# Eight lists of tiles in place of six, and three chains of a scan and two expert layers rearranged between VectorE, ScalarE and GpSimd

## The chip, the cores and the metric

The kernel runs on one core of a Trainium2 chip. The metric is the device time of one execution in microseconds (us), the median of several runs. TensorE (PE) does matrix products, VectorE (DVE) and ScalarE (ACT) elementwise work and the emptying of PSUM, GpSimd (POOL) the scatters of rows, SyncE (SP) issues the other transfers.

## The reference

Three stages follow each other over 2 sequences of 5056 positions with 256 features, 10,112 rows in all. All is float32.

```python
log_a = c * sig_r * np.log(np.clip(a_base, 1e-06, 1.0 - 1e-06))[None, None, :]
a_t = np.exp(log_a)
norm = np.sqrt(np.maximum(1.0 - a_t * a_t, 1e-06))
x_gated = norm * sig_i * x
for t in range(S):
    h = a_t[:, t] * h + x_gated[:, t]
    y[:, t] = h
...
logits = x @ w_gate + modality_bias[modality_id]
e_idx = np.argmax(logits, axis=1)
...
for e in range(E):
    h = np.maximum(x[mask] @ w1[e], 0.0)
    out[mask] = gate_w[mask, None] * (h @ w2[e])
```

The second expert layer is the same without the modality bias. Each has 8 experts of 256 x 1024 and 1024 x 256, and each row goes to one expert; `gate_w` is that expert's softmax probability.

## The kernel before

The scan goes in ten chunks of 512 positions (the last has 448). For a chunk, two halves of 128 features lie on the partitions, and each step runs per half `k` and sequence `b`: ScalarE takes tanh of both gates (L413), the decay (L416), its square (L425) and the root (L433); VectorE clamps in between (`rest`, L430), forms the gated input (`gated`, L419), multiplies it by the root (`mul`, L436) and scans (`scan`, L440). TensorE then turns each of the eight tiles of 128 tokens and multiplies it by the router's weights in the same pass (`rows`, L461), into one of two PSUM buffers. `copy` (L471 on ScalarE, L473 on VectorE; the list `act` says which tile goes to ScalarE) brings the tile's row to SBUF, and `take` (L481) adds the two partial logits of each expert. `route` picks the expert (`pick`, L341) and the place among that expert's tokens (`rank`, L359, with products on TensorE), and `send` (L494) scatters each row, with its number and gate, to the expert's region of a DRAM tensor X1 by an indirect DMA from GpSimd (L219).

Layer 1 works in slots, one for each 256 rows of one expert. A slot loads its rows (`load_rows`), turns them (`transposes`, L904; the copies L905 and L906 make a high and a low half), and runs six points: four of `ffn1` (L915 to L917, emptied by ScalarE as hTh, L919, and by VectorE as the low half hTl, L920) and two of `ffn2` (L929 to L931). Three PSUM buffers `ph` serve `ffn1`. After it, `end_steps` scales the rows by the gate (L941), routes them for layer 2 with `pick` and `rank`, and scatters them to X2. Its steps stand beside the next slot's points. Where the slot two before had another expert, the weights come from DRAM into a ring of five stages and are split into high and low halves (`split`, L878 and L879) during the slot before; there are two weight sets, for even and odd slots. Layer 2 has the same slots without routing.

Which expert a slot serves is settled on the chip. `phases` cuts layer 1 into lists: after so many chunks (`CUTS`) as many slots are listed as whole tiles are sure to be there. `plan_steps` is the plan of a list, 29 small steps of VectorE that count whole tiles for each expert and give each slot its expert, its first row and whether the weights change. Layer 1 has 40 regular slots.

The order is written out by hand. A slot has six ticks, the first slot begins at tick 45 (`T0`), and `STEPS` gives for each chunk the ticks, counted from its start, at which its steps are recorded; what is marked early stands ahead of the slot's point, the rest behind it. The starts of the first three chunks are given. The loop over lists gives the others: a list's last chunk must be sent before its first slot's rows are loaded, chunks keep 12 ticks apart, and starts that are left are spread evenly:

```python
s = max(start[-1] + PACE, LOAD2 + 2 if c + i == 2 else 0, start[c - 1] + (by - start[c - 1]) * (i + 1) // n)
start.append(next(x for x in [s - d for d in range(POINTS)] + [s + d for d in range(POINTS)] if x - start[-1] >= PACE and fits(x, c + i) and x >= LOAD2 + 2))
```

## Time and profile before

| what | value |
|---|---|
| median of 3 runs | 1179.78 us (1169.88 to 1182.34) |
| the profiled execution | 1184.67 us |
| its span in the trace | 1182.9 us |
| TensorE at work | 1093.8 us |
| mean granted TensorE clock | 0.968 of full speed |
| moved by DMA | 133.76 MB |

A row of busy times gives a stretch of the span, its length, and for PE, PEld (the loading of weights into TensorE), DVE, ACT and POOL the busy us with the number of instructions; then the granted clock, the mean busy share of the DMA engines and GB/s. Where a row is of some instructions alone, engines without any are left out. A row of waits says which engine, tensor and line stood idle, and after the arrow what ended it. Durations overlap a little where short instructions follow each other.

### The profile page before, as it was taken

The page shows a single profiled execution, that of the slowest core. Times are in us where ns is not written, and L with a number is a line of the kernel's source. Part 1 is how long each engine was busy: PE and PEld are TensorE (multiplying, and loading weights), DVE is VectorE, ACT ScalarE, POOL GpSimd, SP SyncE. Part 2 cuts the span into 40 slices and gives each one's busy share as a digit, 9 for nine tenths or more (in the row PEclk, how much of TensorE's full clock was granted, in tenths as well). Part 3 has the DMA queues.
Part 4 walks back from the last instruction along what each step waited for, and adds up shares of the span by engine and source line. Part 5 has one row for each costly group of instructions (what it writes and reads, how often), then busy time and mean ns, then how long its engine had stood idle before and what let it go on. Part 6 is the DMA issues. An engine that isn't in the chain of part 4 may idle for free. (4 is left out here: it accounts for less than half of the span.)

```text
span 1182.9 us, 27884 instructions
## 1 busy us (share of the span) xinstructions
PE 1093.8 (92%) x9112; PEld 1073.6 (91%) x9112; DVE 690.7 (58%) x1981; ACT 512.9 (43%) x817; POOL 296.8 (25%) x378
## 2 busy tenths in 40 slices
PE   4287988888899999999999899999999999999997
PEld 2286988888899899989999899999999999999997
DVE  6777878877777877665456644333534643334372
ACT  7745666537363725223234324222524542224362
POOL 2422241444142424141111221211121211111122
PEclk9688989999899999999999899999999999999999
DMA  7766554355333212141114333113332431113350
GB/s 241 238 141 232 185 170 145 121 188 175 107 103 117 96 56 74 38 145 51 38 56 147 101 94 117 46 46 117 116 114 81 137 113 47 46 51 109 119 179 26
DMA packets 71313, 133.76 MB, mean 113 GB/s; under 512 B 11804, under 2 KB 39459, under 8 KB 71106
## 3 DMA queue, kind: packets, MB, share of 16 engines
q1 hardware_dynamic: 59250, 100.20, 27.5%
q0 software_dynamic: 11856, 31.25, 7.4%
q8 instruction: 75, 1.23, 0.5%
q14 instruction: 132, 1.08, 0.3%
HBM read 95.49 MB, written 37.04 MB: 112 GB/s over the span
## 5 line engine op out<-in xcount | busy, mean ns | idle before, releaser
L929 PE MATMUL po<-w2h,hTh 128*128 128x256 f32 (+1 forms) x1344 | 394.9, 294 | 2.8 <-issue 1.5
L915 PE MATMUL ph<-xh,w1h 128*128 128x256 f32 x1312 | 376.0, 287 | 22.8 <-DVE hTl L920 7.8
L931 PE MATMUL po<-w2h,hTl 128*128 128x256 f32 (+1 forms) x1344 | 385.1, 287 | 6.2 <-DVE xl L906 2.5
L930 PE MATMUL po<-w2l,hTh 128*128 128x256 f32 (+1 forms) x1344 | 384.0, 286 | 4.1 <-DVE w2l L879 2.5
L916 PE MATMUL ph<-xl,w1h 128*128 128x256 f32 x1312 | 370.6, 283 | 5.2 <-DVE xl L906 5.2
L917 PE MATMUL ph<-xh,w1l 128*128 128x256 f32 x1312 | 370.6, 282 | 0.0
L920 DVE SCALAR_TENSOR_TENSOR hTl<-ph,hTh 128x512 fp32r<-128x512 f32 x336 | 231.2, 688 | 217.8 <-ACT hTh L919 129.1
L919 ACT ACTIVATE hTh<-ph 128x512 fp32r<-128x512 f32 x336 | 199.2, 596 | 341.2 <-PE ph L917 274.6
L915 PEld LDWEIGHTS ph<-xh,w1h 128*128 128x128 f32 x1312 | 253.3, 193 | 25.8 <-DVE hTl L920 8.9
L931 PEld LDWEIGHTS po<-w2h,hTl 128*128 128x128 f32 x1344 | 257.8, 192 | 9.5 <-DVE hTl L920 3.8
L930 PEld LDWEIGHTS po<-w2l,hTh 128*128 128x128 f32 x1344 | 258.1, 192 | 4.1 <-DVE w2l L879 2.7
L929 PEld LDWEIGHTS po<-w2h,hTh 128*128 128x128 f32 x1344 | 258.0, 192 | 3.8 <-issue 2.2
L916 PEld LDWEIGHTS ph<-xl,w1h 128*128 128x128 f32 x1312 | 251.1, 191 | 5.4 <-DVE xl L906 5.4
L917 PEld LDWEIGHTS ph<-xh,w1l 128*128 128x128 f32 x1312 | 250.3, 191 | 0.0
L219 POOL DMA_INDIRECT out_dram<-orow,xr x88 | 92.5, 1052 | 411.3 <-ACT orow L941 363.6
L941 ACT ACTIVATE orow<-po,xr 128x256 f32<-128x256 f32 x124 | 58.0, 473 | 253.5 <-PE po L931 238.0
L219 POOL DMA_INDIRECT X<-orow,rib x80 | 81.0, 1012 | 216.6 <-DVE lgb L960 53.1
L946 DVE TENSOR_SCALAR orow<-po,xr 128x256 f32<-128x256 f32 x44 | 21.3, 483 | 131.2 <-PE po L931 130.3
L219 POOL DMA_INDIRECT X<-row,ria x79 | 87.0, 1102 | 24.9 <-issue 20.3
L461 PE MATMUL ps<-wI,it 128*128 128x136 f32 x280 | 48.3, 296 | 20.2 <-DVE it L440 15.7
L461 PEld LDWEIGHTS ps<-wI,it 128*128 128x128 f32 x280 | 39.0, 196 | 24.3 <-ACT rt L413 11.1
L906 DVE TENSOR_TENSOR xl<-pt,xh 128x512 fp32r<-128x512 f32 x82 | 55.8, 680 | 2.0 <-ACTq L793 1.3
(171 smaller groups left out, 1012.3 us busy)
## 6 DMA issues: line engine op xcount, KB each, us to landing
stage<-in_wA SPq DMA_DIRECT2D x76, 512.0 KB
xr<-X SPq DMA_DIRECT2D x84, 258.0 KB
rt<-in_rT SPq DMA_DIRECT2D x18, 512.0 KB
it<-in_iT SPq DMA_DIRECT2D x18, 512.0 KB
xt<-in_xT SPq DMA_DIRECT2D x18, 512.0 KB
X<-zr SPq DMA_DIRECT2D x17, 258.0 KB
it<-in_wB SPq DMA_DIRECT2D x4, 512.0 KB
out_dram<-orow,xr POOLq DMA_INDIRECT x88
```

What stands on the lines that cost most here:

```text
L219: i = G.indirect_dma_start(out=dst, out_offset=bass.IndirectOffsetOnAxis(ap=idx, axis=0), in_=rows, in_offset=None, bounds_check=bound, oo ...
L461: PE.matmul(p[:, k * (P + E):(k + 1) * (P + E)], l[:, k, :], wI[:, k, :], start=True, stop=True)
L906: V.tensor_tensor(out=sl.t("xl")[:], in0=p[:], in1=sl.t("xh")[:].bitcast(F32), op=ALU.subtract)
L915: PE.matmul(p[:, j, :], h1[:, k, cs], sl.t("xh")[:, k, :], start=k == 0, stop=False)
L916: PE.matmul(p[:, j, :], h1[:, k, cs], sl.t("xl")[:, k, :], start=False, stop=False)
L917: PE.matmul(p[:, j, :], l1[:, k, cs], sl.t("xh")[:, k, :], start=False, stop=k == KD - 1)
L919: A.activation(hh[:], p[:], func=ACTF.Relu)
L920: V.scalar_tensor_tensor(out=hl[:], in0=p[:], scalar=0.0, in1=hh[:].bitcast(F32), op0=ALU.max, op1=ALU.subtract)
L929: PE.matmul(p[h][:, :wd], hh, h2[:, c, :wd], start=c == 0, stop=False)
L930: PE.matmul(p[h][:, :wd], hh, l2[:, c, :wd], start=False, stop=False)
L931: PE.matmul(p[h][:, :wd], hl, h2[:, c, :wd], start=False, stop=c == KF - 1)
L941: A.activation(orow[:, h, :D], p[h][:, :D], func=ACTF.Copy, scale=g1[:, h:h + 1])
```

## The change

`CUTS` gets five and seven. With the loop above the chunks' start ticks become 5, 15, 34, 62, 86, 110, 134, 158, 170, 182; before they were 5, 15, 34, 62, 74, 86, 110, 134, 158, 182. Two lists of eight slots become four of four.

Row copies take all 272 columns of a tile (256 and twice 8 partial logits) and go to ScalarE from the third chunk on (in the first two as before). `take` adds the partial logits of four tiles at once, from the copied rows. The clamp becomes a Relu of ScalarE and a max inside the multiply, again from the third chunk on. In routing a ninth column holds the 1e-9 of the softmax, and for layer 2 a ninth column holds the mark of an empty row, which GpSimd now computes; the rank's sum writes whole numbers at once. The two PSUM buffers `po` become one tile of two banks, so that one product serves both halves' logits.

```diff
-CUTS = (1, 2, 3, 4, 6, 8)
+CUTS = (1, 2, 3, 4, 5, 6, 7, 8)
...
-         act=(2,), route=28, rank=34, send=35),
+         route=28, rank=34, send=35),
...
+        exs = {n_: [cp.tile([P, n_, E + 1], F32, name=f"ex{n_}{j}") for j in range(2)] for n_ in (H, 8)}
+        for t_ in exs[H] + exs[8]:
+            V.memset(t_[:], 1e-9)
...
-        def pick(lg, n, mk):
+        def pick(lg, n, mk, real=None):
...
+            wide = dm[:, :, :E] if real is None else dm[:]
...
+            if real is not None:
+                a.append(lambda: G.tensor_scalar(out=dm[:, :, E], in0=real, scalar1=0.0, scalar2=BIG, op0=ALU.is_le, op1=ALU.mult))
+            x = lambda: A.activation(ex[:, :, :E], d[:], func=ACTF.Exp)
+            b = [lambda: V.scalar_tensor_tensor(out=dm[:, :, :E], in0=d[:], scalar=0.0, in1=bt(erev, n), op0=ALU.is_equal, op1=ALU.mult),
+                 lambda: V.tensor_reduce(out=my[:], in_=wide, axis=AX.X, op=ALU.max),
+                 lambda: V.tensor_tensor(out=oh[:], in0=dm[:, :, :E], in1=bc(my[:], E), op=ALU.is_equal)]
-            c = [lambda: V.tensor_reduce(out=g[:], in_=ex[:], axis=AX.X, op=ALU.add),
-                 lambda: V.tensor_scalar(out=g[:], in0=g[:], scalar1=1e-9, scalar2=None, op0=ALU.add),
+            c = [lambda: V.tensor_reduce(out=g[:], in_=ex, axis=AX.X, op=ALU.add),
                  lambda: V.reciprocal(g[:], g[:])]
...
+            def d():
+                with nc.allow_low_precision(reason="whole numbers below 2 ** 24"):
+                    V.tensor_reduce(out=ri[:], in_=wide, axis=AX.X, op=ALU.add)
...
             def rest(k):
-                V.tensor_scalar(out=z("q", k), in0=z("q", k), scalar1=-1.0, scalar2=-1e-6, op0=ALU.add, op1=ALU.min)
+                if ci < 2:
+                    V.tensor_scalar(out=z("q", k), in0=z("q", k), scalar1=-1.0, scalar2=-1e-6, op0=ALU.add, op1=ALU.min)
+                else:
+                    A.activation(z("q", k), z("q", k), func=ACTF.Relu, scale=-1.0, bias=1.0)
...
             def mul(k, b):
-                (G if k * B + b in o.get("pool", ()) else V).tensor_tensor(out=z("i", k)[:, b], in0=z("i", k)[:, b], in1=z("q", k)[:, b], op=ALU.mult)
+                if ci < 2:
+                    V.tensor_tensor(out=z("i", k)[:, b], in0=z("i", k)[:, b], in1=z("q", k)[:, b], op=ALU.mult)
+                else:
+                    V.scalar_tensor_tensor(out=z("i", k)[:, b], in0=z("q", k)[:, b], scalar=0.5e-3, in1=z("i", k)[:, b], op0=ALU.max, op1=ALU.mult)
...
-                    box["rows"].append(s1.tile([P, 4, W], F32, name="row", bufs=3))
+                    box["rows"].append(s1.tile([P, 4, D + 2 * E], F32, name="row", bufs=3))
                 row = box["rows"][j // 4][:, j % 4]
-                src = box["p"][j][:, E:E + D]
-                if j in STEP(ci).get("act", ()):
-                    A.activation(row[:, :D], src, func=ACTF.Copy)
+                if j in STEP(ci).get("act", range(n)):
+                    A.activation(row, box["p"][j], func=ACTF.Copy)
                 else:
-                    V.tensor_copy(row[:, :D], src)
+                    V.tensor_copy(row, box["p"][j])
...
-                V.tensor_reduce(out=box["lg"][:, j, :], in_=pair(box["p"][j]), axis=AX.X, op=ALU.add)
+                if j % 4 == 3 or j == n - 1:
+                    m, row = j % 4 + 1, box["rows"][j // 4]
+                    V.tensor_reduce(out=box["lg"][:, j + 1 - m:j + 1, :], in_=pair(row[:, :m]), axis=AX.X, op=ALU.add)
+                    G.tensor_copy(row[:, :m, E + D].bitcast(I32), ids[:, t0 + j + 1 - m:t0 + j + 1])
...
-                    [lambda h=h: V.tensor_scalar(out=lg[:, h, :], in0=p[h][:, D:WR], scalar1=g1[:, h:h + 1], scalar2=None, op0=ALU.mult)
-                     for h in range(H)] + pa,
-                    [px, lambda: V.tensor_scalar(out=vd[:], in0=g1, scalar1=0.0, scalar2=None, op0=ALU.is_gt)] + pb,
-                    [lambda: V.tensor_tensor(out=oh[:], in0=oh[:], in1=bc(vd[:], E), op=ALU.mult),
-                     lambda: V.tensor_scalar(out=vb[:], in0=vd[:], scalar1=-BIG, scalar2=BIG, op0=ALU.mult, op1=ALU.add)],
+                    [lambda: V.tensor_tensor(out=lg[:], in0=sl.t("po")[:, :, D:WR], in1=bc(g1, E), op=ALU.mult)] + pa,
+                    [px] + pb,
+                    [],
...
-                    rb + [lambda: V.tensor_tensor(out=ri[:], in0=r[:], in1=vb[:], op=ALU.add), send]]
+                    rb + [send]]
```

The order of VectorE's instructions at the start of layer 1's slot 9, where a chunk's rows are turned, before (`rib` is the place of a routed row, `lgb`, `mxb`, `db`, `vdb`, `dmb` are the steps of its routing; `lg` and `row` belong to a chunk):

```order
L968 TENSOR_TENSOR rib<-rb,vbb 128x2
L960 TENSOR_SCALAR lgb<-po,xr 128x8 x2
L348 TENSOR_REDUCE mxb<-lgb 128x2
L349 TENSOR_TENSOR db<-lgb,mxb 128x16
L481 TENSOR_REDUCE lg<-ps 128x8
L473 COPY row<-ps 128x256
L920 SCALAR_TENSOR_TENSOR hTl<-ph,hTh 128x512
L962 TENSOR_SCALAR vdb<-xr 128x2
L490 TENSOR_TENSOR lg<-lg,mbs 128x64
L351 SCALAR_TENSOR_TENSOR dmb<-db,cst 128x16
```

And at the same place now:

```order
L393 TENSOR_REDUCE rib<-dmb 128x2
L979 TENSOR_TENSOR lgb<-po,xr 128x16
L358 TENSOR_REDUCE mxb<-lgb 128x2
L359 TENSOR_TENSOR db<-lgb,mxb 128x16
L939 SCALAR_TENSOR_TENSOR hTl<-ph,hTh 128x512
L460 SCALAR_TENSOR_TENSOR it<-rt,carry,it 128x512
L363 SCALAR_TENSOR_TENSOR dmb<-db,cst 128x2x8
L456 SCALAR_TENSOR_TENSOR it<-qt,it 128x512
L364 TENSOR_REDUCE myb<-dmb 128x2
```

The row's copy and reduce are gone, as are the second logit product and the validity test; the scan of the one chunk that is under way stands nearer.

ScalarE in slot 24, before (`orow` are the slot's rows, `exb` its exponentials, `qt` the chunk's squares):

```order
L941 ACTIVATE orow<-po,xr 128x256 x2
L919 ACTIVATE hTh<-ph 128x512
L350 ACTIVATE exb<-db 128x16
L919 ACTIVATE hTh<-ph 128x512 x2
L779 TENSOR_LOAD tj_7708
```

And now, at the same place:

```order
L960 ACTIVATE orow<-po,xr 128x256 x2
L490 ACTIVATE row<-ps 128x272
L938 ACTIVATE hTh<-ph 128x512
L447 ACTIVATE qt<-qt 128x2x448
L362 ACTIVATE ex_159<-db 128x2x8
L490 ACTIVATE row<-ps 128x272
L938 ACTIVATE hTh<-ph 128x512
L447 ACTIVATE qt<-qt 128x2x448
L490 ACTIVATE row<-ps 128x272
L938 ACTIVATE hTh<-ph 128x512
```

Row copies of one chunk and the clamps (L447) of the next now stand between the slot's own evictions.

GpSimd between two slots, before (`X_87` is X2):

```order
L219 DMA X_87<-orow,rib 82944x258 x2
L779 TENSOR_LOAD tj_3418
L793 COMPARE_AND_BRANCH
L793 UNCONDITIONAL_BRANCH x2
L965 COPY orow<-xr 128x2
```

And now:

```order
L219 DMA X_87<-orow,rib 82944x258 x2
L361 TENSOR_SCALAR dmb<-xr 128x2
L798 TENSOR_LOAD tj_3251
L812 COMPARE_AND_BRANCH
L812 UNCONDITIONAL_BRANCH x2
```

The mark of empty rows (L361) stands behind the two scatters of the slot before; VectorE's max `myb` (L364 above) reads it.

## Rows read from the trace of the kernel before

**Rows 1.** the page's first part, busy us (share of the span) xinstructions

```profile
PE 1093.8 (92%) x9112; PEld 1073.6 (91%) x9112; DVE 690.7 (58%) x1981; ACT 512.9 (43%) x817; POOL 296.8 (25%) x378
```

**Rows 2.** by stage: length, busy us per engine, clock, DMA share, GB/s

```profile
99.70:304.90 205.20, 181.84 (x1442) 174.44 (x1442) 162.45 (x580) 119.01 (x175) 69.37 (x96) 0.93 0.48 157
304.90:524.00 219.10, 211.84 (x1851) 208.68 (x1849) 158.32 (x601) 97.63 (x165) 76.53 (x111) 1.00 0.31 96
524.00:644.80 120.80, 120.78 (x1041) 120.28 (x1042) 63.19 (x253) 39.46 (x80) 23.66 (x40) 1.00 0.22 66
644.80:1182.90 538.10, 526.17 (x4458) 525.31 (x4455) 238.77 (x370) 196.89 (x320) 97.06 (x95) 0.99 0.29 93
```

**Rows 3.** busy time by slot, two slots with a weight reload, columns as above

```profile
131.70:144.70 13.00, 12.75 (x123) 12.50 (x122) 12.17 (x41) 11.07 (x17) 2.45 (x3) 1.00 0.30 102
...
280.10:304.90 24.80, 18.00 (x106) 16.40 (x105) 21.94 (x69) 16.96 (x23) 10.08 (x12) 0.81 0.28 97
```

**Rows 4.** TensorE waits, 99.7 to 304.9 us: total us, times, longest

```profile
PE ph L915 <- DVE pbb L380: 5.4, 2, 4.8
PE ps L368 <- DVE oh L353: 2.7, 1, 2.7
PE po L931 <- DVE xl L906: 2.5, 1, 2.5
```

**Rows 5.** VectorE groups, 130 to 510 us: xcount, busy us, mean ns, idle

```profile
L440 DVE TENSOR_TENSOR_SCAN it<-rt,carry,it 128x512 f32<-128x512 f32 x24 | 30.7, 1281 | 1.6 <-DVEq L793 0.4
L473 DVE COPY row<-ps 128x256 f32<-128x256 f32 x55 | 22.8, 415 | 0.1
...
L436 DVE TENSOR_TENSOR it<-it,qt 128x512 f32<-128x512 f32 x24 | 16.3, 678 | 0.7 <-DVEq L793 0.5
L419 DVE SCALAR_TENSOR_TENSOR it<-it,xt 128x512 f32<-128x512 f32 x23 | 15.7, 684 | 3.5 <-DVEq L793 3.2
...
L481 DVE TENSOR_REDUCE lg<-ps 128x8 f32<-128x16 f32 x55 | 9.2, 166 | 11.6 <-PE ps L461 7.6 <-DVEq L793 2.5 <-PE po L930 0.8
L430 DVE TENSOR_SCALAR qt<-qt 128x1024 f32<-128x1024 f32 x12 | 8.5, 708 | 0.0
...
L962 DVE TENSOR_SCALAR vdb<-xr 128x2 f32<-128x2 f32 x25 | 4.5, 180 | 0.0
```

**Rows 6.** ScalarE: a 1024-column pass (130 to 510 us); row copies, ns min/median/max

```profile
L425 ACT ACTIVATE qt<-rt 128x1024 f32<-128x1024 f32 x12 | 12.7, 1057 | 0.7 <-ACTq L793 0.4
...
L471 ACT ACTIVATE row<-ps x7: 379/383/393, 22.9 to 113.9; 128x256 f32<-128x256 f32 x7
```

**Rows 7.** splits L879 alone (DVE, POOL, clock, DMA); three layer-2 slots

```profile
99.70:145.00 45.30, 10.01 (x10) 0.00 (x0) 0.99 0.53 177
...
248.00:304.90 56.90, 10.01 (x10) 0.00 (x0) 0.89 0.48 157
304.90:640.00 335.10, 0.00 (x0) 0.00 (x0) 1.00 0.27 83
...
920.20:932.00 11.80, 11.80 (x103) 11.80 (x101) 8.38 (x10) 7.03 (x11) 2.38 (x2) 1.00 0.63 202
932.00:943.70 11.70, 11.70 (x102) 11.70 (x101) 8.38 (x10) 7.02 (x10) 2.36 (x2) 1.00 0.16 46
943.70:955.40 11.70, 11.70 (x101) 11.70 (x100) 3.85 (x6) 3.27 (x7) 2.00 (x3) 1.00 0.67 224
```

**Rows 8.** timeline, VectorE and GpSimd: start us, length, engine, line

```profile
230.41 0.16 DVE L352 TENSOR_REDUCE myb<-dmb 128x2 f32<-128x16 f32 x1
...
230.48 0.99 POOL L219 DMA_INDIRECT X<-orow,rib  x1 [0.30 <-issue]
...
395.75 0.99 POOL L219 DMA_INDIRECT X<-row,ria  x1 [0.28 <-issue]
...
399.68 1.28 POOL L219 DMA_INDIRECT X<-row,ria  x1 [0.30 <-issue]
```

**Rows 9.** TensorE waits, 304.9 to 524 us, the costliest group

```profile
PE po L931 <- DVE hTl L920: 1.6, 3, 0.7
```

More of the change, by code (lines that the diff above doesn't have):

```diff
@@ L348, in pick @@
             a = [lambda: V.tensor_reduce(out=mx[:], in_=lg, axis=AX.X, op=ALU.max),
                  lambda: V.tensor_tensor(out=d[:], in0=lg, in1=bc(mx[:], E), op=ALU.subtract)]
-            x = lambda: A.activation(ex[:], d[:], func=ACTF.Exp)
-            b = [lambda: V.scalar_tensor_tensor(out=dm[:], in0=d[:], scalar=0.0, in1=bt(erev, n), op0=ALU.is_equal, op1=ALU.mult),
-                 lambda: V.tensor_reduce(out=my[:], in_=dm[:], axis=AX.X, op=ALU.max),
-                 lambda: V.tensor_tensor(out=oh[:], in0=dm[:], in1=bc(my[:], E), op=ALU.is_equal)]
@@ L356, in pick, with rank @@
+            c = [lambda: V.tensor_reduce(out=g[:], in_=ex, axis=AX.X, op=ALU.add),
                  lambda: V.reciprocal(g[:], g[:])]
-            return oh, g, a, x, b, c
-        def rank(oh, n, bs, mk, place):
-            pb, r = mk("pb", [P, n, E], F32), mk("r", [P, n], F32)
+            return oh, g, dm, wide, a, x, b, c
+        def rank(oh, n, bs, dm, wide, ri, place):
+            pb = dm[:, :, :E]
             box = []
@@ L496, in send @@
                     m = min(4, n - j)
[L497 to L498 removed]
+                    G.tensor_copy(box["rows"][j // 4][:, :m, E + D + 1], box["g"][:, j:j + m])
+                scatter(1, X1[:], box["rows"][j // 4][:, j % 4, E:E + W], box["ri"][:, j:j + 1], E * R - 1)
             def warm(box_, n_):
@@ L521, in chunk_at @@
                 at(s + o["rows"][j], lambda j=j: rows(j), early=True)
+                at(s + o.get("copies", o["rows"])[j], lambda j=j: copy(j), early=True)
                 at(s + o.get("takes", o["rows"])[j], lambda j=j: take(j), early=True)
-                at(s + o.get("copies", o["rows"])[j], lambda j=j: copy(j), early=True)
                 at(s + o["send"] + j // 2, lambda j=j: send(j))
@@ L923, in ffn2 @@
             _, _, h2, l2 = wset[sl.ws]
-            p = [sl.t(f"po{h}") for h in range(H)]
+            p = [sl.t("po")[:, h] for h in range(H)]
             wd = WR if sl.layer == 1 else D
@@ L936, in end_steps @@
                 return [[]] * 6
-            p, xr, orow = [sl.t(f"po{h}") for h in range(H)], sl.t("xr"), sl.t("orow")
+            p, xr, orow = [sl.t("po")[:, h] for h in range(H)], sl.t("xr"), sl.t("orow")
             g1 = xr[:, :, D + 1]
@@ L1067, in maybe_steps @@
             some = [Slot(pi, s, 2, sp, (1, 4), "c") for s in range(L, K)]
-            for n_ in "xr st stw xh xl orow lg d dm ex oh pb mx my g r vd vb ri".split():
+            for n_ in "xr st stw xh xl orow lg d dm oh mx my g ri".split():
                 some[0].ring(n_)
```

37 lines of the change are left out of this document (17 added, 20 removed).

## Prediction

> **What bounds the kernel now.** I read the page's busy shares first: TensorE is at work for 1093.8 us, 92% of the span, VectorE for 690.7 [rows 1]. So only what makes TensorE wait, or lowers its clock, can be gained, and I looked for where that is with the busy times by stage, cut at the transposes (L904) that begin each slot's work on TensorE [rows 2]. The last two stages are full: 10 slots of layer 1 without scan in 120.8 us, 12.08 each, with no idle time, and layer 2 with 526.2 busy of 538.1. What comes before 99.7 us is the start, whose transfers the change leaves as they are. Between lie the two stages in which the scan runs beside layer 1. Slots 14 to 29 take 219.1 us for 16, 13.7 each, at clock 1.00; slots 2 to 13 take 205.2 us for 12, 17.1 each, at clock 0.93, with 23.4 us idle. That is the loss: at 13.7 each the twelve would take 164.3, so 40.9 us lie there.
>
> The two stages differ in how close the chunks lie. By the start ticks (six ticks a slot) chunks 3, 4 and 5 begin at 62, 74 and 86, two slots apart, the later ones every four. In the slots of the close stretch TensorE waits longest for VectorE: for the router's ranks (5.4 us, holding a buffer that the next expert matmuls want), for the one-hot tile (2.7), for the low half of a tile (2.5) [rows 4]. VectorE has 162.5 us of work there, 13.5 a slot, more than the 12.08 that TensorE needs. A slot with both chunk work and a weight reload takes 24.8 us, with VectorE at work for 21.9, TensorE 6.8 us idle and the clock at 0.81; another with a reload takes 13.0, VectorE being at work for 12.2 of it [rows 3].
>
> **Part 1, the lists.** CUTS gets 5 and 7, so the lists of eight slots become four of four. The rules for the start ticks then give 62, 86, 110, 134, 158, 170, 182 for chunks 3 to 9 where they gave 62, 74, 86, 110, 134, 158, 182. So the name promises more than it does: three chunks still begin two slots apart, but they are the last three, in slots 19 to 26, and no longer the first.
> Early stage: about one chunk less in slots 2 to 13. I price it as the spaced stage, 164.3, and add what that stage has none of: four weight reloads (slots 2, 4, 11, 13; the splits L879 take 10.0 us of VectorE from 99.7 to 145 us and 10.0 from 248 on [rows 7]). A reload costs between nothing (13.0) and 24.8 - 13.7 = 11.1; I take 3 each, nearer the cheap end since the dear one coincides with a scan, so 176.3. Gain: 205.2 - 176.3 = 28.9.
> Late stage: three effects. First, the three close chunks. Nine slots of the close stretch today (144.7 to 304.9) cost 160.2 against 123.3 at 13.7; the excess of 36.9 is the upper end, nothing the lower. Which of them it is depends on VectorE's load, worked out under part 2: I take 1 us for each of the six fullest slots, 6.
> Second, more reloads. From the inputs that the reference draws with its seed only experts 4 and 6 are ever chosen in layer 1. After five to eight chunks they have 2588/2532, 3084/3060, 3578/3590 and 4110/4082 tokens. In tiles of 256 the lists at five and six chunks get two of each and fit the two weight sets; the list at seven gets one of expert 4 and three of 6, the one at eight three and one. That changes the expert for slots 26, 27, 28 and 29. The same count for the kernel before gives reloads at 4, 11 and 13 and none later, and the trace has no split from 304.9 to 640 us [rows 7]. Four reloads bring 8 MB of loads and 4 x 5.0 us of VectorE. Layer 2 bears two in a row without loss: 11.8 and 11.7 us, as a slot with none, while VectorE goes from 3.9 to 8.4 [rows 7]. The last chunk's arithmetic is over by slot 26, so I take 0.5 each, 2 in all; the bounds are 0 and 4 x 11.1 = 44.
> Third, two more plans of 29 small instructions, some 5 us of VectorE each at the 0.17 of such a one (L962 in [rows 5] is the nearest), in slots with room; nothing.
>
> **Part 2, shorter chains.** Per chunk from the third on VectorE loses 8 copies of 0.415 us, 2 clamps of 0.708, 6 of 8 row reduces of 0.166 (the two left cover 4 rows each), a cast and an add of about 0.17 [rows 5]: 3.3 + 1.4 + 0.9 + 0.3 = 6.0 us. The multiply becomes a three-operand form; the nearest row for it, the gating (L419), takes 0.684 against 0.678, so nothing. Per slot of layer 1 the validity test, two masks, the add before the reciprocal and the add on the rank go (the pattern is L962, 0.18, five of them) and one of two logit products of about the same: 1.1 us. ScalarE takes 8 copies of about 0.39 and two passes of 1.06 [rows 6]: 5.2 us a chunk.
> So the late stage's VectorE: 158.3 now, less 4.5 chunks x 6.0 and 16 slots x 1.1, plus 7 for half a chunk more (gating, multiply and scan are 4 x (0.684 + 0.678 + 1.281) = 10.6 of a whole one), 20 for reloads, 10 for plans: about 151, 9.4 a slot, as today. ScalarE's: 97.6, plus 4.5 x 5.2, some 7 for the half chunk and 4 x 4 passes of 1.06 for the reloads, about 145 or 9.1 a slot, somewhat less than in the early stage today (119.0 for 12). There TensorE's longest waits are all for VectorE [rows 4]. That is why I take the close chunks near the cheap end. The waits that VectorE still causes in the late stage, 1.6 us for the costliest group [rows 9], should shrink: -2.
> VectorE: DVE Perf Modes in the Trainium skill (section The perf-mode tier table) speaks against moving the clamp: a fp32 tensor_scalar in SBUF goes at two elements a cycle, a tensor_tensor at one. The trace agrees: 1024 columns in 0.708 us by the clamp, 512 in 0.678 by the multiply [rows 5]. By that rule VectorE gives up its cheapest pass for a dearer one, 14 x (1.06 - 0.71) = 4.9 us, and were ScalarE the bound the sum would end near 1167.
>
> **Part 3, new waits.** (a) The row copy of a chunk's fifth tile reuses a buffer whose four scatters the chunk before has just issued. That wait stood on VectorE; now it stands on ScalarE, ahead of the expert evictions (hTh) for which VectorE and then TensorE wait. It bites only where chunks lie two slots apart, at chunks 8 and 9. Four scatters take from 395.75 to 400.96 us (the last begins at 399.68 and takes 1.28) [rows 8], while the copy wants the buffer two ticks after the first; 0 to 5 us each. TensorE can run on with two other buffers: 2.5 each, 5 in all. (b) The mark for empty rows moves to GpSimd, behind the two scatters of the slot before, and VectorE's second max waits for it. In the rows shown that max starts at 230.41 and the second scatter ends at 231.47 [rows 8], so it is 1.1 us later at least, and I take 1.4 with GpSimd's own instruction; in 18 of 38 slots of layer 1, counted in the same timeline, the two are within 0.3 us or in this order. Behind it on VectorE stands the next hTl. In slots that have VectorE idle it costs nothing, in the 18 at most 1.4, 25 us; spare VectorE time hides it, I take 0. It can gain nothing. The PSUM pair of one tile instead of two is read before it is written again four points later: nothing.
> Start: the chunk-0 route loses some 1 us of VectorE chain; -1, though xt's landing may hide that.
>
> **Sum.** -28.9 + 6 + 2 - 2 + 5 - 1 = -18.9. The profiled execution took 1184.7 us, 4.9 above the median of 1179.8, so the sum gives 1166 on its own terms and 1161 from the median; I say 1162, near the latter, since the changed kernel is judged by a median too.
>
> **Rivals.**
> 1. The loss moves with the close chunks: ScalarE, which has the passes of one chunk and the copies of another in each of slots 22 to 25, replaces VectorE as the engine that TensorE waits for, and the late stage pays the 36.9 less 6 for two reloads = 31 instead of 11. Then -28.9 + 31 + 2 - 2 - 1 = +1, wait (a) being within the 31: 1181 from the median, as the others here. For it: wait (a) and the table loads; against it: the waits shown are for VectorE [rows 4, 9].
> 2. Slower: the reloads of slots 26 to 29 cost what slot 13 does, 44 instead of 2, because the loads queue on SP behind row loads that wait for a list: -18.9 + 42 = +23, 1203. It turns slower than before from about 5.2 us a reload ((18.9 + 2) / 4). Against it: layer 2's reloads in a row are free.
> 3. The early stage keeps half its loss, since its DMA share of 0.48 (0.31 late) and not VectorE sets it, by late loads and slow issue: a gain of 14.5 there in place of 28.9, so -4.5 in all, 1175.
> 4. Everything that is left of the waits goes, and both scan stages run at 13.1 a slot, with 2 us for each early reload: -40 early, -9 late, 1131. For it: the six slots' 6 us and the 2.5 us a copy are my choices above their lower end, nothing; against it: the spaced stage stands at 13.7 today with VectorE as lightly loaded.
>
> **How the numbers follow.** Forecast 0.50, its own range 1150 to 1174; rivals 0.16, 0.10, 0.12, 0.12. A measurement tells about 1% from no change, so faster is below 1168: most of the forecast (0.44), rival 4 and a little of rival 3, 0.58. Within 1%: rest of the forecast, rivals 1 and 3, 0.31. Slower: rival 2 and a tail, 0.11. The range runs from half-way to rival 4 to rival 1, 1145 to 1183.
>
> **What would show it.** Right: slots 2 to 13 near 176 us at a clock of 0.97 or more, the router's wait gone from TensorE's list; VectorE's busy total down by some 60 us; splits (L898 after) in the slots before 26 to 29, with those slots at 13 to 15 us; ScalarE waiting for row scatters at two tiles. Wrong: slots 2 to 13 above 190, or slots 22 to 29 with TensorE waiting for ScalarE's row copies or the low halves of new weights, at a clock below 0.95.

## The result, and the profile after

The changed kernel is slower: 1189.9 us median (1186.7 to 1191.9) against 1176.4 (1169.9 to 1182.3) in the same comparison, a ratio of 1.0102 with an interval of [1.0063, 1.0141]. In a later comparison on another chip the ratio was 1.0067 [1.0040, 1.0093]. The forecast was 1162, faster by 1.5%; the sign was wrong.

The page's busy totals after, which answer to [rows 1]:

```profile
PE 1094.4 (92%) x9112; PEld 1076.7 (91%) x9112; DVE 647.7 (54%) x1670; ACT 560.9 (47%) x915; POOL 304.3 (26%) x418
```

VectorE lost 43 us of work (690.7 to 647.7), not 60, ScalarE gained 48, and TensorE's work is what it was. By stage, cut at the transposes (now L923) of slots 2, 14, 25, 31 and 40, columns as in [rows 2] (a slot's transposes stand in the slot before it, ahead of most splits of its weights, so the late splits for slot 26 lie in the stretch of slot 26):

```profile
105.80:286.37 180.57, 168.72 (x1393) 165.38 (x1393) 121.55 (x399) 115.38 (x187) 62.14 (x96) 0.95 0.45 145
286.37:437.39 151.02, 148.38 (x1310) 146.62 (x1309) 104.03 (x345) 102.22 (x168) 53.02 (x84) 1.00 0.36 116
437.39:540.93 103.54, 85.22 (x696) 82.78 (x695) 67.28 (x217) 46.13 (x85) 45.27 (x61) 0.93 0.57 166
540.93:649.51 108.58, 108.58 (x939) 108.12 (x938) 50.40 (x178) 34.99 (x73) 23.59 (x45) 1.00 0.22 67
```

The early stage is shorter (180.6 against 205.2) and slots 14 to 24 are as before; slots 25 to 30 are the loss, 103.5 us where the kernel before took 80.6 between its own transposes of slots 25 and 31. One slot a row, 25 to 29:

```profile
437.39:454.91 17.52, 14.02 (x118) 13.52 (x117) 11.35 (x45) 7.54 (x14) 9.45 (x12) 1.00 0.66 199
454.91:473.64 18.73, 15.96 (x142) 14.99 (x141) 13.21 (x43) 11.20 (x21) 3.32 (x9) 1.00 0.47 143
473.64:493.95 20.31, 15.41 (x115) 15.27 (x113) 11.17 (x30) 7.81 (x17) 14.21 (x19) 0.83 0.63 191
493.95:506.27 12.32, 12.32 (x120) 12.27 (x119) 9.76 (x29) 8.15 (x14) 2.11 (x3) 1.00 0.55 156
506.27:526.26 19.99, 12.85 (x106) 12.11 (x104) 17.34 (x59) 8.09 (x14) 13.76 (x18) 0.97 0.79 219
```

In slots 25 to 27 VectorE, ScalarE and GpSimd all have time left, so it is not one engine's load that makes them long: something comes late. (In slot 29 VectorE has 17.3 of 20.0 us.) What TensorE waits for in slots 25 to 30 (total us, times, longest), where [rows 9] had 1.6 us at most:

```profile
PE ps L481 <- ACT row L490: 7.8, 2, 4.9
PE pt L923 <- DMA xr<-X: 3.5, 1, 3.5
PE ph L934 <- DVE dmb L395: 2.2, 1, 2.2
PE po L950 <- DVE hTl L939: 2.2, 3, 1.5
PE ps L481 <- DVE base L389: 1.0, 1, 1.0
```

The chain behind the first of these can be followed in the timelines of VectorE, GpSimd and ScalarE through slot 26, which begins at 454.91 (start, length, engine, line; in brackets the idle time before and who ended it):

```profile
460.81 1.22 DVE L898 TENSOR_TENSOR w1l<-stage,w1h 128x1024 fp32r<-128x1024 f32 x1
...
465.09 2.36 DVE L898 TENSOR_TENSOR w2l<-stage,w2h 128x1024 fp32r<-128x1024 f32 x2 [0.47 <-ACT w2h L897]
...
468.17 0.22 DVE L393 TENSOR_REDUCE ria<-dm 128x8 int32<-128x64 f32 x1
468.31 0.16 DVE L393 TENSOR_REDUCE rib<-dmb 128x2 int32<-128x18 f32 x1
...
472.40 0.99 POOL L219 DMA_INDIRECT X<-orow,rib  x1 [2.06 <-issue]
473.39 0.27 POOL L361 TENSOR_SCALAR dmb<-xr 128x2 f32<-128x2 f32 x1
...
473.69 0.17 DVE L364 TENSOR_REDUCE myb<-dmb 128x2 f32<-128x18 f32 x1 [3.68 <-POOL dmb L361]
...
474.06 1.06 POOL L219 DMA_INDIRECT X<-row,ria  x1 [0.28 <-POOL row L516]
...
482.18 0.40 ACT L490 ACTIVATE row<-ps 128x272 f32<-128x272 f32 x1 [8.57 <-DMA X<-row,ria]
```

The low halves of a reload (L898) stand on VectorE ahead of the rank chain; the rank of chunk 8 (`ria`) and of the slot (`rib`) come at 468.2, GpSimd scatters the slot's rows, then the mark, then chunk 8's rows from 474.06 on; ScalarE, holding chunk 9's fifth row copy, waits 8.6 us for them, and TensorE behind it. Chunk 8's own fifth copy had waited 5.2 us in the same way in slot 25, ahead of any late reload.

### The profile page after: what moved, and what is told of

Its sections match the earlier page's. It is cut to its first block, busy times and chain, and to the rows that moved or that the text cites. A ratio compares the mean times of both kernels' runs of the same rounds, so it can differ in the third digit from the quotient of the medians.

```text
span 1189.2 us, 27803 instructions
## 1 busy us (share of the span) xinstructions
PE 1094.4 (92%) x9112; PEld 1076.7 (91%) x9112; DVE 647.7 (54%) x1670; ACT 560.9 (47%) x915; POOL 304.3 (26%) x418
## 5 line engine op out<-in xcount | busy, mean ns | idle before, releaser
L934 PE MATMUL ph<-xh,w1h 128*128 128x256 f32 x1312 | 376.7, 287 | 25.5 <-DVE dmb L395 6.4
L934 PEld LDWEIGHTS ph<-xh,w1h 128*128 128x128 f32 x1312 | 254.4, 194 | 28.2 <-issue 11.2
L935 PEld LDWEIGHTS ph<-xl,w1h 128*128 128x128 f32 x1312 | 252.1, 192 | 6.0 <-DVE xl L925 5.1
L219 POOL DMA_INDIRECT out_dram<-orow,xr x88 | 86.8, 986 | 419.2 <-ACT orow L960 375.9
L960 ACT ACTIVATE orow<-po,xr 128x256 f32<-128x256 f32 x124 | 54.4, 472 | 279.9 <-PE po L950 268.5
L219 POOL DMA_INDIRECT X<-row,ria x79 | 90.9, 1150 | 24.2 <-issue 17.8
L481 PEld LDWEIGHTS ps<-wI,it 128*128 128x128 f32 x280 | 39.2, 198 | 21.5 <-ACT rt L427 10.8
L898 DVE TENSOR_TENSOR w1l<-stage,w1h 128x1024 fp32r<-128x1024 f32 x46 | 55.8, 1219 | 4.7 <-ACT w1h L897 4.3
```

The source lines that it names most:

```text
L219: i = G.indirect_dma_start(out=dst, out_offset=bass.IndirectOffsetOnAxis(ap=idx, axis=0), in_=rows, in_offset=None, bounds_check=bound, oo ...
L481: PE.matmul(p[:, k * (P + E):(k + 1) * (P + E)], l[:, k, :], wI[:, k, :], start=True, stop=True)
L898: by.tensor_tensor(out=l, in0=src, in1=h.bitcast(F32), op=ALU.subtract)
L934: PE.matmul(p[:, j, :], h1[:, k, cs], sl.t("xh")[:, k, :], start=k == 0, stop=False)
L935: PE.matmul(p[:, j, :], h1[:, k, cs], sl.t("xl")[:, k, :], start=False, stop=False)
L960: A.activation(orow[:, h, :D], p[h][:, :D], func=ACTF.Copy, scale=g1[:, h:h + 1])
```

## The experiments

Ratios are to the kernel before in the same batch. The batches ran on different chips (the kernel before took 1179.8, 1181.5, 1164.6 and 1168.3 us), so times are compared within a batch. e1, e2, e4 and e5 ran on chip 10, e7 to e10 on chip 6, e11 to e14 on chip 2, e15 to e17 on chip 7; the chip of the first two profiles is not on record. The lengths of slots 25 to 30 agree better: 103.5 and 100.4 for the changed kernel, 80.6 and 81.6 for the one before. A difference of 3 us there between runs on two chips says nothing.

| kernel | ratio, interval | slots 2–13 | 14–24 | 25–30 |
|---|---|---|---|---|
| before (first profile) | 1 | 205.2 | 150.6 | 80.6 |
| changed (first profile) | 1.0102 [1.0063, 1.0141] | 180.6 | 151.0 | 103.5 |
| e1 free rows | 1.0025 [1.0006, 1.0044] | 187.7 | 151.7 | 96.7 |
| e2 no list at seven | 0.9939 [0.9915, 0.9963] | 185.1 | 161.8 | 82.6 |
| e4 chains alone | 0.9934 [0.9912, 0.9955] | 191.9 | 148.7 | 80.1 |
| e5 lists alone | 1.0078 [1.0048, 1.0108] | 187.1 | 155.9 | 102.4 |
| e7 no late reloads | 0.9840 [0.9796, 0.9885] | 188.9 | 150.1 | 88.3 |
| e8 three slots apart | 1.0146 [1.0097, 1.0195] | 203.8 | 167.6 | 80.6 |
| e9 no low halves | 1.0009 [0.9977, 1.0042] | 190.4 | 151.8 | 93.9 |
| e10 mark on VectorE | 1.0101 [1.0064, 1.0138] | 194.8 | 156.8 | 101.1 |
| e11 loads, no splits | 0.9867 [0.9846, 0.9889] | 178.2 | 150.1 | 85.0 |
| e12 free rows, no reloads | 0.9842 [0.9819, 0.9865] | 175.4 | 151.2 | 83.2 |
| e13 list at nine | 1.0078 [1.0058, 1.0099] | 180.8 | 148.3 | 94.6 |
| e14 low halves on GpSimd | 1.0232 [1.0209, 1.0255] | 181.4 | 150.6 | 117.4 |
| e15 no high halves | 1.0089 [1.0068, 1.0110] | 181.6 | 150.3 | 101.0 |
| e16 changed, again | 1.0067 [1.0040, 1.0093] | 175.9 | 151.7 | 100.4 |
| e17 before, again | 0.9997 [0.9978, 1.0016] | 194.8 | 149.4 | 81.6 |

**The two parts of the change, one at a time.** e4 is the changed kernel with the old lists, e5 the kernel before with the new ones.

```diff
-CUTS = (1, 2, 3, 4, 5, 6, 7, 8)
+CUTS = (1, 2, 3, 4, 6, 8)
```

> The changed kernel with the old lists (six of them, chunks 3, 4 and 5 two slots apart, no reload after slot 13), so the shorter chains alone. Theory A: the scatter waits of ScalarE appear at chunks 4 and 5 instead, and the early stage gains little, 5 to 10 us against the kernel before, while slots 14 to 29 gain 3 to 5 us: ratio 0.990. Theory B: with no reloads late the whole gain of the chains shows, 15 us or more: 0.987 or less. The start: if the chains are what makes slots 0 and 1 6 us longer, they are 54 us here too; if that was the run's chance, 48 to 50.

> The kernel before with the new lists alone. Theory A: the copies are on VectorE, so the scatter waits stand there; slots 25 and 27 lose less than in the changed kernel, since ScalarE's evictions run on, the early stage gains 20 us or more, and the time is at or below the kernel before: 0.985 to 1.0. Theory B: the reloads cost the late stage what they do in the changed kernel, 20 us and more with the longer chains: 1.005 to 1.02. Start: 48 us if the chains are what lengthens it.

The chains gain 0.7%, the lists lose 0.8%: the wrong sign is the lists'. The product is 0.9934 x 1.0078 = 1.001; the two together measured 1.0102 and 1.0067, so some 0.6 to 0.9%, 7 to 11 us, come from their meeting. By the profiles it does not lie in the late slots: over slots 14 to 30 the chains alone gain 2.4 us, the lists alone lose 27.1, both together lose 23.4. In slots 0 to 13 the chains alone gain 11.7 us (253.1 to 241.4) and the lists 19.6 (to 233.5), but both only 18.5 (to 234.6; this and the 253.1 are of the first profiles). The likely reason, not tested by itself, is that the lists take away the close chunks from which the chains had their gain there. On top of the new lists the chains thus bring nothing that shows (1.0078 against 1.0067 and 1.0102). e4 is faster than both kernels.

**The scatter wait.** e1 gives the fifth to eighth row of the last two chunks a free gate buffer in place of the ring of three.

```diff
-box["rows"].append(s1.tile([P, 4, D + 2 * E], F32, name="row", bufs=3))
+if ci >= NC - 2 and j == 4:
+    t_ = s1.tile([P, KD, B, CH], F32, name="rt", bufs=2)[:].rearrange("p k b s -> p (k b s)")
+    box["rows"].append(t_[:, :4 * (D + 2 * E)].rearrange("p (j c) -> p j c", j=4))
+else:
+    box["rows"].append(s1.tile([P, 4, D + 2 * E], F32, name="row", bufs=3))
```

> The changed kernel, but the second row tile of chunks 8 and 9 lies in a gate buffer that is free by then, so its copy waits for no scatter; nothing else differs. Theory A (the late loss is ScalarE's wait for the scatters of the chunk before: 5.2 and 8.6 us in the trace of the changed kernel, with 2.9 and 4.9 us of TensorE idle and a low clock behind the second): both waits are gone and slots 25 and 27 fall from 17.5 and 20.3 us to about 14.5, some 9 us in all, time 0.992 of the changed kernel. Theory B (the four weight reloads): the waits are gone but slots 26 to 29 stay at 71 us together, gain under 3 us. Theory C (the close chunks as such): the gap moves to the next wait, gain under 3 us.

Slots 25 and 27 fell to 13.3 and 13.1 us, 11.4 together, but slot 28 rose from 12.3 to 17.4, so slots 25 to 30 gain 6.8 (3.7 against the changed kernel's 100.4) and are still 16 us longer than before: most of the loss is not this wait. Nor did the chains bring it: e5, whose copies are on VectorE, has it there, ahead of the same copy, and takes 102.4 us for slots 25 to 30:

```profile
485.58 0.43 DVE L473 COPY row<-ps 128x256 f32<-128x256 f32 x1 [5.30 <-DMA X<-row,ria]
```

e1's ratio of 1.0025 is near the product of the parts, but these runs give no reason why it should be.

**Without the list at seven.** e2 drops the 7 from `CUTS`.

> The changed kernel without the list at seven chunks: the starts of the chunks stay the same, the list at eight has eight slots, four of each expert, so that no slot from 14 on changes its weights and one plan of 29 steps is gone. Theory B (reloads): slots 26, 27, 29 and 30 lose most of their 23 us over the kernel before, 12 to 18 us gained, and 8.4 MB less is moved. Theory A (scatters): the two waits of ScalarE stay at 5 us and more, and the gain is 3 to 8 us, of slots 26 and 29 alone. Theory C: no gain beyond 5 us of VectorE work that was hidden.

0.9939, and slots 25 to 30 are back at 82.6. But, other than I expected, the starts did not stay: without the 7 the rules give chunks 3 to 9 the starts 62, 86, 110, 122, 134, 158, 182: the three close chunks move to the middle, where slots 14 to 24 pay 161.8 in place of 151.0. So e2 took away reloads and close late chunks at once. The next runs part them.

**Reloads out, chunks where they are.** e7 leaves loads and splits out in slots 23 to 30, e11 only the splits, e9 only VectorE's part of the splits, e15 only ScalarE's.

```diff
-            when(sl, sl.f, body)
+            if sl.pi not in (6, 7):
+                when(sl, sl.f, body)
...
-            when(sl, None if sl.always else sl.f2, body)
+            if sl.pi not in (6, 7):
+                when(sl, None if sl.always else sl.f2, body)
```

That is e7; e11 has the second half of it. Both also lose the jumps around the splits, on ScalarE, VectorE and GpSimd. Slots 23 to 25 have the jumps and no reload: with them they take 45.6 to 46.9 us (the changed kernel, e9 and e15), in e7 and e11 45.3 and 45.2, so the jumps are worth 0.4 to 1.7 us there; in slots 26 to 30 they were not taken out by themselves. e9, and the same around the activation for e15:

```diff
-                by.tensor_tensor(out=l, in0=src, in1=h.bitcast(F32), op=ALU.subtract)
+                if sl.pi not in (6, 7):
+                    by.tensor_tensor(out=l, in0=src, in1=h.bitcast(F32), op=ALU.subtract)
```

> The changed kernel, same lists and same chunk starts, but the slots of the lists at seven and at eight chunks (23 to 30) leave out their weight reloads, loads and splits both; the tokens of slots 26 to 29 then go through another expert's weights. Theory B (the reloads themselves are what the late stage pays): slots 25 to 30 fall from 103.5 us to about 83, the time from 1190 to about 1170. Theory C (three chunks two slots apart are what it pays, reloads or not): they stay above 97, the time above 1183. Theory D (the two only hurt together, a reload being harmless in a slot without chunk work): also near 83 here; D is told from B by the kernel with spread chunks.

> The changed kernel with the loads and ScalarE's high halves of those reloads kept, but VectorE's low halves (five subtractions, 5.1 us a reload) left out in the lists at seven and eight; those slots then use old low halves. If VectorE's block of subtractions, standing ahead of the rank chain and the low halves hTl, is what a late reload costs: within 3 us of the kernel without any reload, some 1172. If the loads (8 MB on the queue that also brings the rows) or ScalarE's passes are: within 5 us of the changed kernel, 1185 or more. In between: both, in that proportion.

> The changed kernel with the loads of the weights kept in the lists at seven and eight, but their splits left out altogether (ScalarE's high halves and VectorE's low halves): slots 26 to 29 then use old weights. Slots 25 to 30 took 103.5 us with everything, 93.9 without VectorE's part, 88.3 without loads and splits. If the loads on SP's queue cost the 5.6 us that VectorE's part left: slots 25 to 30 stay near 94. If ScalarE's passes do: near 88. Layer 2 may take some 10 us less, as in the run without reloads, since other weights choose other experts; the slots 25 to 30 decide, not the time.

> The changed kernel with VectorE's low halves kept but ScalarE's high halves (five passes, 4 x about 1.1 us and a short one) left out in the reloads of the lists at seven and eight; the weights of slots 26 to 29 are then wrong. Slots 25 to 30 took 103.5 us with both, 93.9 without VectorE's part, 85.0 without either. If the two parts add: ScalarE's is about 9, so 94 to 95 here. If ScalarE's passes cost only because VectorE's subtractions wait for them: 88 or less. If VectorE's block alone makes the delay and the other run's saving came from elsewhere: 100 or more.

Busy times of slots 25 to 30 of e9:

```profile
436.94:530.88 93.94, 83.32 (x697) 80.93 (x695) 49.51 (x197) 45.82 (x85) 38.80 (x61) 0.96 0.61 183
```

of e11:

```profile
423.67:508.69 85.02, 79.95 (x696) 79.21 (x695) 48.74 (x197) 29.86 (x65) 37.91 (x61) 0.98 0.64 200
```

of e15:

```profile
427.20:528.20 101.00, 84.24 (x697) 81.83 (x696) 67.52 (x217) 29.95 (x65) 44.95 (x61) 0.95 0.57 170
```

and of the changed kernel on e15's chip (e16):

```profile
423.50:523.90 100.40, 84.92 (x696) 82.63 (x695) 67.12 (x217) 46.11 (x85) 45.11 (x61) 0.95 0.58 171
```

No price of the loads can be seen: e11 moves 200 GB/s there and is the shorter of e11 and e7, though on another chip. The splits cost the rest: 100.4 (e16) less 85.0 is 15.4 for four reloads; other pairs of runs with and without give 12 to 18 (on one chip, e10 less e7, 12.8). VectorE's 19 us of low halves alone (67.5 less 48.7 at work) keep the price whole, 101.0; ScalarE's 16 (45.8 less 29.9) alone keep 6 to 9 of it, 93.9 against the 88.3 of e7 on the same chip and the 85.0 of e11. The parts do not add up: either makes the chain late. My expectation of 94 for e15 was wrong; e7 and e9 came out between their two figures, e7 nearer the one for reloads. Of the 15.4 us some 10 are TensorE standing idle and 5 are its own work going slower: the same products take 84.9 us at a mean clock of 0.95 in e16 and 79.95 at 0.98 in e11. (The times of e7 and e11 fall by another 10 us, since layer 2 gets shorter: 528.7 and 529.1 us against 539.7. Rows that went through other weights choose other experts there, and their traces have one slot fewer. Slots 25 to 30 come before that.)

How e11 differs in the chain, from GpSimd's and VectorE's timelines of its slot 26, which begins at 440.81:

```profile
447.02 0.22 DVE L393 TENSOR_REDUCE ria<-dm 128x8 int32<-128x64 f32 x1
...
452.90 1.06 POOL L219 DMA_INDIRECT X<-row,ria  x1 [0.28 <-POOL row L516]
```

The rank of chunk 8 stands 6.2 us after the slot's beginning, in the changed kernel 13.3; the first of its scatters 12.1 after it, there 19.2. The seven microseconds go on to the scatters, to the row copy, to TensorE. The other two runs keep the order of their lengths: with ScalarE's part alone (e9, slot 26 from 453.78) the rank stands at 9.0, with VectorE's alone (e15, from 444.72) at 13.2:

```profile
462.74 0.22 DVE L393 TENSOR_REDUCE ria<-dm 128x8 int32<-128x64 f32 x1
```

and

```profile
457.91 0.22 DVE L393 TENSOR_REDUCE ria<-dm 128x8 int32<-128x64 f32 x1
```

ScalarE's wait for chunk 8's scatters, 8.6 us in the changed kernel, is shorter in e11:

```profile
460.35 0.40 ACT L490 ACTIVATE row<-ps 128x272 f32<-128x272 f32 x1 [5.66 <-DMA X<-row,ria]
```

**The wait by itself.** e12 is e1 without the late reloads.

> The kernel with the free row buffer for the last two chunks' second four tiles, and without the reloads (loads and splits) of the lists at seven and eight. The free buffer alone took 8.3 us off the changed kernel, 6.8 in slots 25 to 30. If ScalarE's wait for the scatters has a price of its own: it takes as much off here, slots 25 to 30 from 88.3 to 80 to 82. If the wait is long only because the reloads make the scatters late: 1 to 3 us, 85 to 88.

83.2 us, between the two expectations: 5.0 below e7, which ran on another chip, and 1.8 below e11, which ran on the same one but has the loads. So the wait has a price of its own of 2 to 5 us, and of 4 to 7 with the reloads (e1). Whether the price grows with them is not settled by these lengths; the wait itself does.

**The mark for empty rows** back on VectorE (e10).

```diff
-a.append(lambda: G.tensor_scalar(out=dm[:, :, E], in0=real, scalar1=0.0, scalar2=BIG, op0=ALU.is_le, op1=ALU.mult))
+a.append(lambda: V.tensor_scalar(out=dm[:, :, E], in0=real, scalar1=0.0, scalar2=BIG, op0=ALU.is_le, op1=ALU.mult))
```

> The changed kernel with the mark for empty rows computed by VectorE again instead of GpSimd, so that VectorE's second max no longer waits behind the scatters of the slot before; VectorE gets one small instruction of about 0.2 us a slot back. If that wait (3.7 us seen once after slot 26) costs what the late stage lost: slots 25 to 30 fall by 5 to 10 us, the time to 1180 to 1185. If it stands beside other waits: within 2 us of the changed kernel, 1188 to 1192; if VectorE's load in the whole of layer 1 decides, up to 4 us slower.

No gain: slots 25 to 30 are 2.4 us shorter than in the first profile (0.7 longer than in e16), slots 14 to 24 5.8 longer, and the ratio is the changed kernel's. The 3.7 us wait is real in the timeline and stands beside others.

**No close chunks.** e13 adds a list at nine chunks, which spreads the last starts to 158, 182, 206. e8 goes without the 7 and writes the starts out three slots apart.

```diff
-CUTS = (1, 2, 3, 4, 5, 6, 7, 8)
+CUTS = (1, 2, 3, 4, 5, 6, 7, 8, 9)
```

```diff
-CUTS = (1, 2, 3, 4, 5, 6, 7, 8)
+CUTS = (1, 2, 3, 4, 5, 6, 8)
...
-START = (5, 15, 34)
+START = (5, 15, 34, 62, 80, 98, 116, 134, 158, 182)
```

> The changed kernel with one more list, at nine chunks: by the rules chunks 8 and 9 then begin at 182 and 206 and every chunk from the third on comes four slots after the one before; slots 31 to 34 come from the new list, the reloads of slots 26 to 29 stay. If close chunks (with the scatter wait) are 8 to 17 us of the late stage and reloads beside spaced chunks still cost 3 to 4 us each: slots 14 to 39 fall by 8 to 15 us, the time to 1175 to 1182. If the reloads cost only where chunks are close: 1164 to 1170. If the new list brings reloads of its own in slots 31 to 35, or its own 29 instructions hurt: up to 15 us more than the first figure.

> The changed kernel with the list at seven chunks left out (so no late reloads) and the start ticks of chunks 3 to 9 written out as 62, 80, 98, 116, 134, 158, 182, so that no two chunks begin nearer than three slots. The version without the list at seven but with three chunks two slots apart ran at 1173.6, its slots 14 to 24 at 161.8 us against 151.0. If the close chunks cost those 11 us: slots 14 to 24 near 152, slots 2 to 13 near 185, the time 1161 to 1166. If only the number of chunks in a stretch counts, not their spacing: 1171 to 1175, with the loss spread over slots 5 to 20.

e13 is no better than the changed kernel (1.0078): slots 14 to 30 take 242.9 us against 252.1 in e16, but slots 31 to 39 take 115.9 against 108.6, for the list at nine brings four reloads of its own, in slots 34 to 37. So it came out by the third of its expectations. Its slots 26 to 29, all with a reload's splits and now beside spaced chunks, and then slots 34 to 37, which have them with no chunk beside them (the last scatter of a chunk begins at 548.6):

```profile
437.26:452.97 15.71, 14.70 (x127) 14.45 (x126) 11.62 (x30) 10.23 (x19) 2.26 (x6) 1.00 0.68 230
452.97:466.48 13.51, 13.51 (x118) 13.46 (x117) 9.98 (x27) 7.07 (x14) 4.76 (x10) 1.00 0.56 169
466.48:483.84 17.36, 14.75 (x123) 14.03 (x122) 12.63 (x37) 15.37 (x24) 3.13 (x8) 0.90 0.61 201
483.84:503.95 20.11, 14.94 (x106) 14.51 (x105) 18.07 (x55) 10.91 (x16) 17.38 (x14) 0.84 0.24 74
558.07:572.44 14.37, 13.86 (x105) 13.63 (x106) 8.03 (x18) 8.39 (x14) 1.69 (x3) 0.88 0.79 255
572.44:584.81 12.37, 12.34 (x107) 12.12 (x106) 9.39 (x22) 8.00 (x14) 2.58 (x6) 1.00 0.74 235
584.80:597.30 12.50, 12.39 (x107) 12.15 (x106) 9.38 (x22) 8.07 (x14) 2.71 (x6) 1.00 0.69 213
597.29:609.59 12.30, 12.27 (x107) 12.05 (x106) 10.35 (x25) 7.44 (x13) 2.57 (x6) 1.00 0.34 105
```

The four slots before the first four, at the same ticks of a chunk and without a reload, took 14.76, 13.51, 12.54 and 13.48. So a reload cost 0.9, 0.0, 4.8 and 6.6 us, 12.3 in all against 15.4 beside the close chunks: it is not the closeness that makes them dear. Slots 34 to 37 cost 2.3, 0.3, 0.4 and 0.2 (a slot with neither takes 12.1, a ninth of the 108.58 above); slot 34 comes behind an idle of TensorE and at a clock of 0.88. Slot 34 aside, a reload is nearly free without a chunk and in the two slots of a chunk's row copies. It is dear in the third, where ScalarE has a chunk's passes (15.4 us of work), and in the fourth, where VectorE has its scans (18.1); that these passes and scans, ahead of the ranks, are what makes it dear is read from the order of the instructions and was not tried.

e8 was a miss on both its readings, the slowest but one. Three slots apart is worse than two apart thrice: slots 2 to 24 take 371.4 against 346.9 in e2 (on another chip) and 342.1 in e9 on the same one. In its timeline (ScalarE, VectorE) the slot's output rows wait 11 us, and the routing 7 behind them, at the time when GpSimd issues a chunk's eight row scatters ahead of the slot's two:

```profile
223.39 0.84 ACT L960 ACTIVATE orow<-po,xr 128x256 f32<-128x256 f32 x2 [10.96 <-remote]
...
224.26 0.17 DVE L979 TENSOR_TENSOR lgb<-po,xr 128x16 f32<-128x16 f32 x1 [7.27 <-ACT orow L960]
```

That this order is the cause was not tried by itself.

**A cure that failed.** e14 gives the low halves of the two lists to GpSimd.

```diff
             h1, l1, h2, l2 = wset[sl.ws]
+            if sl.pi in (6, 7):
+                by = 'GGGG'
```

> The changed kernel with the low halves of the reloads in the lists at seven and eight computed by GpSimd instead of VectorE; nothing is left out. VectorE's part was worth 9.6 us of slots 25 to 30. If VectorE's time ahead of the rank chain was the cost: slots 25 to 30 at 94 to 98, the time some 5 us below the changed kernel. If GpSimd, which issues the scatters, becomes the late one: no gain or a loss, 103 to 115.

117.4 us, more than the range given for the loss: GpSimd takes 2.38 us for a subtraction of 1024 columns where VectorE takes 1.22, itself waits for ScalarE's high halves, and the scatters stand behind it. From the first to the last of chunk 8's eight scatters it is 21.0 us, in the changed kernel 10.5. From GpSimd's timeline:

```profile
463.70 0.98 POOL L219 DMA_INDIRECT X<-row,ria  x1 [0.30 <-DVE hTl L941]
464.83 2.37 POOL L900 TENSOR_TENSOR w1l<-stage,w1h 128x1024 fp32r<-128x1024 f32 x1
...
474.39 2.37 POOL L900 TENSOR_TENSOR w1l<-stage,w1h 128x1024 fp32r<-128x1024 f32 x1 [4.42 <-ACT w1h L899]
477.17 1.01 POOL L219 DMA_INDIRECT X<-row,ria  x1 [0.28 <-POOL row L516]
```

**Before and after on one chip.**

> The changed kernel as it is, to be profiled on the same chip as the kernel before. If the gain in the early stage is what the two first profiles showed (24.6 us in slots 2 to 13, 18.5 in slots 0 to 13) and not one chip's: slots 0 to 13 are 17 to 24 us shorter than the kernel before's on this chip, slots 14 to 30 some 23 us longer, the ratio 1.005 to 1.015. If part of the gain was the chip's: below 15 us.

> The kernel before as it is, profiled on the same chip: ratio 1.00 within its interval; slots 0 to 13 at 240 to 255 us, slots 14 to 30 at 230 to 233.

Slots 2 to 13 of the kernel before:

```profile
95.15:289.90 194.75, 174.19 (x1441) 168.81 (x1441) 161.41 (x580) 118.98 (x175) 77.42 (x98) 0.96 0.53 173
```

and of the changed one:

```profile
95.95:271.80 175.85, 163.75 (x1394) 159.25 (x1393) 121.75 (x404) 117.47 (x191) 59.85 (x94) 0.99 0.50 162
```

The gain is 18.9 us there (18.2 from slot 0 on), the loss 2.3 in slots 14 to 24 and 18.8 in slots 25 to 30; with 2.7 in layer 2 and 0.7 in the start the spans differ by 5.5 (1167.4 to 1172.9). That is what e16 expected; for e17 slots 0 to 13 came out just short, at 238.9.

## Why the prediction was wrong, by its steps

**Part 1, the early stage: right in place and level, 10 us too large as a gain.** The forecast was 176.3 us at a clock of 0.97 or more; the changed kernel took 175.9 at 0.99 on the last chip. But the same chip gave the kernel before 194.8, not 205.2. The first profile held some 10 us that are not the close chunks' but go with the chip, as the last section shows (slots 5, 9 and 13 took 19.6, 19.1 and 24.8 us, on the last chip 15.4, 15.8 and 21.1): taking them for the change's was the fault. The first changed profile's 180.6 also stands behind a start 6 us longer than before; over slots 0 to 13 it too gains only 18.5 (234.6 against 253.1). TensorE's wait for the ranks, which was to go, is still in its list for these slots, 3.0 us in the first profile and 3.9 in e16 (L934 <- dmb L395). The price of 3 us a reload was wrong one by one: slots 4 and 11 took 12.4 and 13.3, nothing, slot 13 still 19.9.

**Part 1, the late stage: "Layer 2 bears two in a row without loss ... The last chunk's arithmetic is over by slot 26, so I take 0.5 each" failed.** The four reloads cost 15.4 us, 3.9 each (3.0 to 4.6 by the pair of runs), not 2 in all. Number, slots and size in bytes (8.5 MB more moved) were right, and nothing speaks against the transfers being free. What was over by slot 26 was only the scan. Rows, row copies, routing, ranks and scatters of chunks 8 and 9 run through slots 26 to 29, the splits of ScalarE and VectorE stand in front of these, and the lateness goes down the chain of ranks, scatters and row copies. Layer 2, from which I took the price, has no such chain, and slots 35 to 37 of e13, three reloads in a row at 0.2 to 0.4 each, have only the slot's own part of it. The dear case [rows 3] was in the profile: I kept it as the upper bound, 44.

**Close chunks and the scatter wait** together cost less than the 6 + 5 forecast: slots 25 to 30 take 85.0 (e11) or 88.3 (e7) with them and without splits, 81.6 before, and slots 14 to 24 stay within 2.3 us of before. The wait's own 2 to 5 us are near the 5 of the sum; that it gets longer behind a reload was not in it. **Wait (b)** was taken as 0, and e10 bears that out although VectorE does wait.

**Part 2, the shorter chains: right in sign.** Alone they gain 0.7% (e4), but on top of the lists nothing. The pages' totals for VectorE part the 43 us that came in place of 60: the chains take 66 off (690.7 to 624.4 in e4), the lists put 22 on (712.5 in e5). In slots 14 to 29 the lists' share was right (158.3 to 197.0 in e5, 39 us, where half a chunk, reloads and plans were to add 37) and the chains' too large: 158.3 to 129.2 in e4, 29 us, where 4.5 chunks and 16 slots were to give 45. So VectorE had 166.9 us there, not 151; ScalarE's 145 came out at 145.0. (Small slips in the working: the row reduces of a chunk come to 1.0 us, not 0.9, and the clamps that moved are 16, not 14.)

**Which rival.** The second: reloads of slots 26 to 29, with their place and their point of change (about 5 us each). They cost 3.9, and since the early stage gave 10 less than forecast the sum turns from (18.9 + 2 - 10) / 4 = 2.7 on. It got a chance of 0.10; its stated reason, loads late behind row loads on SP, is not what e11 shows. The first rival wanted 31 us of close chunks, and e11 and e7 leave 3 to 7 for them. The third gave the early stage a gain of 14.5, nearer the 18.9 than the forecast's 28.9; its reason, late loads, no run tested. Of the signs that were to speak against the forecast the late ones were all there (slots 2 to 13 above 190 was not): TensorE waiting for ScalarE's row copies in slots 25 to 27, a clock of 0.93 in that stage, and three of slots 26 to 29 at 18.7 to 20.3 where it said 13 to 15. The Trainium skill's page VectorE: DVE Perf Modes (section The perf-mode tier table) spoke against moving the clamp; no run moves the clamp alone, so what that part was worth is not shown, only that the chains as a whole gain in e4.

What stays open: why the early stage takes longer on some chips, what the clamp's move and the jumps around the late splits are worth alone, and which instructions make the third and fourth slot of a chunk dear. The 2.7 us that layer 2 is longer need no reason: in the runs with all weights right it takes 537.7 to 540.4 us, with little order by kernel.

## What to carry to other kernels

The price of a piece of work is that of its neighbours' chain: five microseconds of VectorE are nearly free in a slot where nothing follows from them and cost up to seven where ranks, scatters and buffers hang on them, so take a price from a slot with the same chain behind it and treat a dear slot in the profile as a case to explain, not as an outer bound. A plan that smooths one stage moves its pressure; count what the new plan makes of the last stage too. Before a gain is read from one profile's stage, ask whether another chip or run shows the same length.
